# K transposed on VectorE and q in a block-diagonal stationary tile, in a decode step of attention and MLP

## The chip, the cores and the metric

One core of a Trainium2 chip runs the whole program. The time is in device microseconds, from one execution; lower is better. Weights and cache start in HBM, and each is read once.

## The reference

One token per sequence for two sequences (B = 2, D = 576). The normed token feeds two branches that are added to it: attention over the last W = 2048 keys of a cache (32 query heads, 16 key heads, head size 128), and an MLP with squared relu (F = 4608). All inputs are bf16.

```python
xn = _layernorm(x)
q = (xn @ wq) as [B, 32, 1, 128]
k, v = k_cache[:, :, Sk - W:, :], v_cache[:, :, Sk - W:, :]   # W = 2048, each key head serves 2 query heads
p = softmax(q k^T * 128 ** -0.5);  o = p v
A = o.reshape(B, 1, 4096) @ wo
h = relu(xn @ w1 + b1) ** 2;  Bout = h @ w2 + b2
return x + A + Bout
```

## The kernel before

The attention is cut into eight units `u`: four key heads of one sequence each (`NU = 8`). A unit has 2 MB of K and 2 MB of V. Both are loaded by one DMA each into a tile of 128 partitions by 8192 bf16: a partition holds 64 consecutive keys of one head (4 heads by 32 partitions). Six such tiles (`kvpool`) rotate over all K and V loads and one piece of w2; a load whose tile is still in use waits on SP's queue, with all that stands behind it. The order of loads is k0, wq, k1, v0, k2, v1, k3, v2, k4, v3, k5, v4, k6, v5, w1, k7, v6, v7, wo, then w2 in pieces (w2a, w2b, three of w2c). wq, w1 and wo share one buffer (`wbig`), so w1 waits for q and wo waits for the MLP's first product.

For each unit, `transposes(u, g)` turns K: g goes over eight groups of 1024 columns, each transposed by TensorE as f32 pairs into PSUM (`kT_ps`, three buffers, L97) and copied out in turn by ScalarE (L270) and VectorE (L272) into `kT`, half a unit (`t` = 0, 1) to a tile, with two buffers. `scores(u, t)` then takes eight matmuls for a half: a stationary tile of 32 columns cut from `qz` (q of the eight query heads with zeros around it), 512 moving columns, on four column groups of TensorE at once (`tile_position`), all summed in `sc_ps`, whose first matmul writes a mask. `softmax(u)` takes the row maximum (L291), picks own heads (L293), takes the maximum over partitions on GpSimd (L295), makes the bias (L298), the exponential on ScalarE (L302) and the transposed probabilities `pT` on VectorE (L305).

`pv(w)` multiplies by V two units later (w = u - 2), 16 matmuls on four column groups; `pv_end(w)` adds four parts of `o_ps` on VectorE (L333, L335), and its `fin` sums over partitions on TensorE (`op_ps`) and finishes in three VectorE instructions (L344, L347, L351) into `ws`. `step(u)` mixes the eight groups of unit u with `pv` of unit u - 2. TensorE's order is the program's order (L94 and L97 are the helpers that record every matmul and transpose, so go by tile names); the other engines are ordered by the scheduler. Step 1 to step 6 follow each other; then `mlp_h` with w1, step 7, `pv_all(6)` and `pv_all(7)`. The closing block sums into `out_ps`: 128 matmuls with wo, 72 with w2a, 36 with w2b and 36 with w2c.

Of the kernel before, what the change touches and what calls it, by code (L numbers as in the profile page):

```python
# [16 lines left out]
def kernel(  # L17
# [14 lines left out]
    nc = tc.nc  # L32
# [17 lines left out]
    JG = 8  # L50
    NG = NJ // JG
# [5 lines left out]
    TG = NG // NT  # L57
    QZ = 2 * NC
    assert SR == 32 and NG % NT == 0
# [35 lines left out]

    def transpose(*a, **k):
        tc.keep_in_program_order(nc.tensor.transpose(*a, **k))  # L97
# [18 lines left out]
    def issue_flat(w, name):  # L116
        n = w.shape[0] * w.shape[1] // P
        tl = wbig.tile([P, NH * L1], BF16, tag="wbig", name=name)
        nc.sync.dma_start(out=tl[:, 0:n], in_=w.rearrange("r n -> (r n)").rearrange("(p l) -> p l", p=P))
        return tl  # L120

    const.tile([P, 144], F32, name="pad_0")
# [15 lines left out]
    tmp_f = work.tile([P, 2, Dh], F32, tag="tmp", name="tmp_f")  # L138
# [50 lines left out]
    nc.vector.tensor_scalar(out=off[:], in0=own[:], scalar1=BIG, scalar2=-BIG, op0=ALU.mult, op1=ALU.add)  # L189
    of_h = const.tile([P, NC * WC], F32, name="of_h")  # L190
# [30 lines left out]
    qz = const.tile([P, NQ, B, 2, 3 * QZ], BF16, name="qz")  # L221
    nc.gpsimd.memset(qz[:], 0.0)
# [3 lines left out]
    def q_block():  # L226
        for t in range(NH):
            for g in range(NG4):
                o = t * LQ + g * QW
                matmul(q_ps[32 * g:32 * g + 2 * B, :], lhsT=xnT[:, t].rearrange("p x b -> p (x b)"),  # L230
                       rhs=wq_sb[:, o:o + QW], start=(t == 0), stop=(t == NH - 1), skip_group_check=True,
                       tile_position=(0, 32 * g))
        row_t = const.tile([RB, 4 * HW], BF16, tag="row", name="qrow")
        qrow = row_t[:, 0:2 * QW]
        nh = QH // 2
        for k in range(2):
            cp = nc.scalar.copy if k else nc.vector.tensor_copy
            cp(out=qrow[:, k * QW:(k + 1) * QW].rearrange("p (i a d) -> p i a d", a=2, d=Dh),  # L238
               in_=q_ps[0:RB, k * QW // 2:(k + 1) * QW // 2].rearrange("p (i d) -> p i d", d=Dh).unsqueeze(2)
               .to_broadcast([RB, nh, 2, Dh]))  # L240
        qrow_f = qrow.bitcast(F32)
        qT_ps = psum.tile([P, QH * P], F32, tag="sc", bufs=2, name="qT_ps")
        for i in range(QH):
            transpose(out=qT_ps[:, i * P:i * P + RB], in_=qrow_f[:, i * Dh:(i + 1) * Dh],
                      identity=ident_f[0:RB, 0:RB])
        qT_v = qT_ps[:].bitcast(BF16).rearrange("p (i g e x b c) -> p b x g c e i", g=NG4 // 2, e=2, x=32 // B, b=B, c=2)
        hd = Dh // 2
        for j2 in range(2):
            cp = nc.scalar.copy if j2 else nc.vector.tensor_copy
            pp = slice(hd * j2, hd * (j2 + 1))  # L250
            o = QZ + NC * j2
            for b in range(B):
                for half in range(2):
                    cp(out=qz[pp, half * NQ // 2:(half + 1) * NQ // 2, b, :, o:o + NC].rearrange(  # L254
                        "p g c (e i) -> p g c e i", e=2), in_=qT_v[pp, b, half])

    kT_tiles, sc_tiles, pT_tiles, o1_tiles, o_tiles = {}, {}, {}, {}, {}
    def transposes(u, g):
        k_f = k_tiles[u][:].bitcast(F32)
        kT_ps = psum.tile([P, JG * P], BF16, tag="kT", bufs=3, name=f"kT_ps_{u}_{g}")  # L260
        kT_f = kT_ps[:].bitcast(F32)
        for i in range(JG // 2):
            j = g * JG // 2 + i
            transpose(out=kT_f[:, i * P:(i + 1) * P], in_=k_f[:, j * P:(j + 1) * P], identity=ident_f[:])
        t, o = divmod(g, TG)
        if o == 0:
            kT_tiles[(u, t)] = ktpool.tile([P, TG * JG * P], BF16, tag="kT_sb", name=f"kT_{u}_{t}")
        kT = kT_tiles[(u, t)][:, o * JG * P:(o + 1) * JG * P]
        if g % 2 == 0:
            nc.scalar.copy(out=kT, in_=kT_ps[:])  # L270
        else:
            nc.vector.tensor_copy(out=kT, in_=kT_ps[:])  # L272

    def scores(u, t):
        tq, b = divmod(u, B)
        if t == 0:
            sc_tiles[u] = psum.tile([P, NJJ * 32], F32, tag="sc", bufs=2, name=f"sc_ps_{u}")
            matmul(sc_tiles[u][:], lhsT=far_h[:], rhs=is_h, start=True, stop=False, skip_group_check=True)
        sc_ps = sc_tiles[u]
        kT = kT_tiles.pop((u, t))[:].rearrange("p (j k c) -> p j k c", k=P, c=2)  # L280
        z = QZ * (1 - t)
        for c in range(2):
            for g in range(4):
                matmul(sc_ps[32 * g:32 * (g + 1), :], lhsT=qz[:, tq, b, c, z:z + SR],
                       rhs=kT[:, :, 32 * g:32 * (g + 1), c], start=False, stop=(t == NT - 1 and c == 1),
                       skip_group_check=True, tile_position=(0, 32 * g))

    def softmax(u):
        sc_ps = sc_tiles.pop(u)
        m1 = work.tile([P, 1], F32, tag="m1", name=f"m1_{u}")  # L290
        nc.vector.tensor_reduce(out=m1[:], in_=sc_ps[:], axis=AX.X, op=ALU.max)  # L291
        m2 = work.tile([P, NC], F32, tag="m2", name=f"m2_{u}")
        nc.vector.tensor_scalar(out=m2[:], in0=off[:], scalar1=m1[:, 0:1], scalar2=None, op0=ALU.add)  # L293
        gmax = work.tile([P, NC], F32, tag="gmax", name=f"gmax_{u}")
        nc.gpsimd.partition_all_reduce(gmax[:], m2[:], channels=P, reduce_op=ReduceOp.max)  # L295
        gown = work.tile([P, NC], F32, tag="gown", name=f"gown_{u}")
        bias = work.tile([P, 1], F32, tag="bias", name=f"bias_{u}")
        nc.vector.scalar_tensor_tensor(out=gown[:], in0=gmax[:], scalar=-scale, in1=own[:], op0=ALU.mult,  # L298
                                       op1=ALU.mult, accum_out=bias[:])
        p_sb = work.tile([P, NJJ * 32], BF16, tag="p_sb", bufs=1, name=f"p_{u}")  # L300
        o1 = keep.tile([P, Dh + 1], F32, tag="o1", name=f"o1_{u}")
        nc.scalar.activation(out=p_sb[:], in_=sc_ps[:], func=ACT.Exp, bias=bias[:, 0:1], scale=scale,  # L302
                             accum_out=o1[:, Dh:Dh + 1])
        pT = keep.tile([P, NJJ, SR], BF16, tag="pT", name=f"pT_{u}")
        nc.vector.transpose(out=pT[:].rearrange("p j r -> p (j r)"), in_=p_sb[:])  # L305
        pT_tiles[u] = pT
        o1_tiles[u] = o1
# [6 lines left out]
    def pv(u, part, parts):  # L314
        n = NJJ // parts
        if part == 0:
            o_tiles[u] = psum.tile([P, NS * Dh], F32, tag="o", name=f"o_ps_{u}")
        v = v_tiles[u][:].rearrange("p (t j s d) -> p j t s d", t=NT, s=2, d=Dh)
        for j in range(part * n, (part + 1) * n):
# [3 lines left out]
        if part == parts - 1:  # L323
            pT_tiles.pop(u)

    def pv_end(u):
# [3 lines left out]
        for k in range(NS):  # L330
            kw = dict(out=o1[:, 0:Dh], in0=o_ps[:, k * Dh:(k + 1) * Dh])
            if k == 0:
                nc.vector.tensor_scalar(scalar1=in_s[:, 0:1], scalar2=None, op0=ALU.mult, **kw)  # L333
            else:
                nc.vector.scalar_tensor_tensor(scalar=in_s[:, k:k + 1], in1=o1[:, 0:Dh], op0=ALU.mult, op1=ALU.add,  # L335
                                               **kw)

        def fin():
# [5 lines left out]
            nc.vector.reciprocal(out=linv[pp, :], in_=op[pp, Dh:Dh + 1])  # L344
            om_t = work.tile([P, Dh], F32, tag="om", name=f"om_{u}")
            om = om_t[pp, :].rearrange("p (q r) -> p q r", r=WR)
            nc.vector.scalar_tensor_tensor(out=om, in0=op[pp, 0:Dh].rearrange("p (q r) -> p q r", r=WR),  # L347
                                           scalar=linv[pp, 0:1], op0=ALU.mult, op1=ALU.mult,
                                           in1=own_c[pp, :].unsqueeze(2).to_broadcast([32, WC, WR]))
            with nc.allow_low_precision(reason="sums of one term and zeros"):  # L350
                nc.vector.tensor_reduce(out=ws[pp, :, BS * b], in_=om.rearrange("p q r -> p r q"), axis=AX.X,  # L351
                                        op=ALU.add)
# [3 lines left out]
    def mlp_h(w1_sb):  # L356
        h_ps = [psum.tile([P, HB], F32, tag="kT", bufs=3, name=f"h_ps_{k}") for k in range(2)]
# [29 lines left out]
    def step(u):  # L387
        fin = None
        w = u - 2
        with_pv = w >= 0  # L390
        for g in range(NG):
            transposes(u, g)
            if with_pv and g == 1:
                pv(w, 0, 2)
            if with_pv and g == 2:
                pv(w, 1, 2)
                fin = pv_end(w)
            if g == TG + 1:
                scores(u, 0)
            if g == TG + 2 and fin:  # L400
                fin()
        scores(u, 1)
        softmax(u)

    def pv_all(u):
        pv(u, 0, 1)
        pv_end(u)()

    for g in range(NG):
        transposes(0, g)  # L410
    q_block()
    for t in range(NT):
        scores(0, t)
    softmax(0)
    load_v(2)
    b1_rows = B_b1.rearrange("(x n) -> x n", n=HW)
# [4 lines left out]
    load_k(4)  # L421
# [16 lines left out]
    nc.sync.dma_start(out=w2a_sb[:], in_=w2_rows[0])  # L438
# [3 lines left out]
    step(NU - 1)  # L442
# [45 lines left out]
```

## Time and profile before

| what | value |
|---|---|
| median of 4 runs | 134.1 us (134.02 to 134.65) |
| the profiled execution | 134.12 us, span 132.2 us |
| mean granted TensorE clock | 0.827 |
| read from HBM | 53.62 MB, 406 GB/s over the span |
| busy, share of the span | TensorE 64%, its weight loads 39%, VectorE 48%, ScalarE 35%, GpSimd 4% |
| K transposes on TensorE (f32, 256) | 39.9 us |
| copies of them | ScalarE 31.9 us, VectorE 21.8 us |
| chain that ended last, by engine | DMA 77%, TensorE 17% |

A group's line reads: line of the code, engine, operation, out<-in, shapes and count; then busy us and mean ns of one; then idle us of the engine just before, with what ended most of it. A timeline line reads: start us, length us, engine, line, operation, tiles, count, and in brackets the idle time before it. The chain's lines have start, length and what. `PEld` is TensorE's weight load, `SPq` the issuing of DMAs.

### The profile page before, as it was taken

To read this page: it belongs to the slowest core of one execution; us is meant where nothing else is said; L and a number is where in the kernel's file an instruction comes from. 1 tells how busy PE (TensorE), PEld (TensorE's weight loads), DVE (VectorE), ACT (ScalarE), POOL (GpSimd) and SP (SyncE) were. 2 spreads that over 40 slices of the span, in tenths; PEclk is the share of its full clock that TensorE was granted. 3 is DMA by queue.
4 is the path that set the end of the run, shared out by engine and by line. 5 is a ranking of instruction groups with operands and counts; after the bars stand their busy time and mean duration, and the time that the engine had idled before them with its cause. 6 is when DMAs were issued, how large, how long until landed. Compare 5 with 4: busy or idle time off the path is not lost.

```text
span 132.2 us, 2285 instructions
## 1 busy us (share of the span) xinstructions
PE 84.0 (64%) x949; PEld 51.4 (39%) x949; DVE 63.0 (48%) x176; ACT 46.7 (35%) x67; POOL 4.9 (4%) x15
## 2 busy tenths in 40 slices
PE   0079219699698779687696597003919974619651
PEld 0068102258345435353353353002418631209550
DVE  7764300325549657677496576400074477560000
ACT  5717300318846366085283563200015452000000
POOL 5000000010010010100100100100000001000000
PEclk9999975556999999999999999955555899755775
DMA  4999989999999999999999999999999999899960
GB/s 159 387 447 469 424 383 431 426 441 426 421 444 411 441 426 426 431 426 446 421 444 411 426 493 401 457 411 394 441 426 436 473 429 457 382 427 401 417 246 1
DMA packets 3511, 53.76 MB, mean 407 GB/s; under 512 B 419, under 2 KB 558, under 8 KB 814
## 3 DMA queue, kind: packets, MB, share of 16 engines
q1 hardware_dynamic: 3456, 53.61, 95.1%
q8 instruction: 7, 0.11, 0.3%
q10 hardware_dynamic: 46, 0.02, 0.0%
q14 instruction: 2, 0.02, 0.0%
HBM read 53.62 MB, written 0.00 MB: 406 GB/s over the span
## 4 chain that ended last, share of the span: by engine, by line
DMA 77%; PE 17%; SPq 2%; DVE 1%; issue 1%; ACT 0%; ACTq 0%; DVEq 0%
DMA w<-in_B_w_dram 25%; DMA w2c<-in_B_w_dram 23%; DMA k<-in_A_k_cache_dram 15%; DMA wq<-in_A_wq_dram 14%; PE kT_ps L97 5%; PE h_ps L94 3%; PE q_ps L94 3%; PE sc_ps L94 2%; PE out_ps L94 1%; PE qT_ps L97 1%; SPq L106 1%; PE o_ps L94 1%; DVE qrow L238 1%; DVE qz L254 0%; SPq L438 0%
## 5 line engine op out<-in xcount | busy, mean ns | idle before, releaser
L97 PE MATMUL kT_ps<-ident_f,k 128*128 128x128 f32 x256 | 39.9, 304 | 6.1 <-DMA k<-in_A_k_cache_dram 4.0
L97 PEld LDWEIGHTS kT_ps<-ident_f,k 128*128 128x128 f32 x256 | 31.5, 156 | 19.4 <-issue 10.7
L270 ACT COPY kT<-kT_ps 128x1024 bf16<-128x1024 bf16 x32 | 31.9, 1013 | 17.3 <-PE kT_ps L97 17.2
L272 DVE COPY kT<-kT_ps 128x1024 bf16<-128x1024 bf16 x32 | 21.8, 681 | 5.7 <-PE kT_ps L97 5.5
L94 PE MATMUL sc_ps<-kT,qz 128*32 128x512 bf16 x128 | 10.5, 414 | 6.4 <-DVE kT L272 4.7
L302 ACT ACTIVATE p<-sc_ps,bias 128x512 bf16<-128x512 f32 x8 | 5.5, 687 | 21.4 <-DVE gown L298 21.3
L94 PE MATMUL o_ps<-v,pT 128*32 128x512 bf16 x128 | 10.9, 423 | 0.0
L94 PEld LDWEIGHTS <-xnT 128*4 128x4 bf16 x108 | 3.5, 121 | 18.0 <-issue 16.4
L94 PE MATMUL h_ps<-w,xnT 128*4 128x288 bf16 x72 | 4.5, 443 | 8.7 <-DMA w<-in_B_w_dram 8.7
L305 DVE STREAM_TRANSPOSE pT<-p 128x512 bf16<-128x512 bf16 x8 | 5.7, 710 | 6.1 <-ACT p L302 6.1
L335 DVE SCALAR_TENSOR_TENSOR o<-o_ps,in_s,o 128x128 f32<-128x128 f32 x24 | 8.3, 346 | 0.4
L291 DVE TENSOR_REDUCE m<-sc_ps 128x1 f32<-128x512 f32 x8 | 5.5, 692 | 5.5 <-PE sc_ps L94 5.5
L375 DVE TENSOR_TENSOR hrow<-t 100x1152 bf16<-100x1152 f32 x2 | 2.6, 1354 | 10.4 <-ACT t L373 10.4
L94 PE MATMUL q_ps<-wq,xnT 128*4 128x512 bf16 x36 | 4.0, 627 | 5.3 <-DMA wq<-in_A_wq_dram 5.3
L295 POOL PARTITION_ALL_REDUCE gmax<-m x8 | 2.9, 367 | 105.8 <-DVE m L293 105.8
L94 PE MATMUL op_ps<-o,of_h 128*32 128x129 f32 x16 | 3.4, 299 | 4.6 <-DVE o L335 4.6
L94 PEld LDWEIGHTS <-qz 128*32 128x32 bf16 x128 | 2.2, 98 | 10.6 <-DVE kT L272 7.2
L456 ACT CAST fin_sb<-out_ps 113x144 bf16<-113x144 f32 x1 | 0.3, 280 | 17.1 <-PE out_ps L94 17.1
L97 PE MATMUL pro_ps<-ident,xn_sb 2*128 2x2 bf16 x5 | 0.9, 181 | 6.8 <-DVE xn_sb L171 6.5
L238 DVE CAST qrow<-q_ps 100x512 bf16<-100x512 f32 x1 | 0.7, 693 | 8.7 <-PE q_ps L94 8.7
L94 PE MATMUL out_ps<-wo,ws 128*17 128x144 bf16 x128 | 4.0, 325 | 1.2 <-DVE ws L351 1.2
L94 PEld LDWEIGHTS <-hT_sb 128*17 128x17 bf16 x144 | 3.4, 109 | 3.2 <-issue 3.1
(71 smaller groups left out, 58.1 us busy)
## 6 DMA issues: line engine op xcount, KB each, us to landing
k<-in_A_k_cache_dram SPq DMA_DIRECT2D x8, 2048.0 KB, 20.9
v<-in_A_v_cache_dram SPq DMA_DIRECT2D x8, 2048.0 KB, 21.0
w<-in_B_w_dram SPq DMA_DIRECT2D x1, 5184.0 KB
wq<-in_A_wq_dram SPq DMA_DIRECT2D x1, 4608.0 KB, 17.9
wo<-in_A_wo_dram SPq DMA_DIRECT2D x1, 4608.0 KB
w2a<-in_B_w_dram SPq DMA_DIRECT2D x1, 2592.0 KB, 26.6
w2b<-in_B_w_dram SPq DMA_DIRECT2D x1, 1296.0 KB
w2c<-in_B_w_dram SPq DMA_DIRECT2D x1, 864.0 KB
```

Of the source, the lines that this page charges most:

```text
L94: tc.keep_in_program_order(nc.tensor.matmul(*a, **k))
L97: tc.keep_in_program_order(nc.tensor.transpose(*a, **k))
L106: nc.sync.dma_start(out=tl[:], in_=cache[b, tq * TH:(tq + 1) * TH, S0:Sk, :].rearrange("h (c j) d -> c h (j d)", c=CP))
L238: cp(out=qrow[:, k * QW:(k + 1) * QW].rearrange("p (i a d) -> p i a d", a=2, d=Dh), in_=q_ps[0:RB, k * QW // 2:(k + 1) * QW // 2].rearrang ...
L270: nc.scalar.copy(out=kT, in_=kT_ps[:])
L272: nc.vector.tensor_copy(out=kT, in_=kT_ps[:])
L291: nc.vector.tensor_reduce(out=m1[:], in_=sc_ps[:], axis=AX.X, op=ALU.max)
L295: nc.gpsimd.partition_all_reduce(gmax[:], m2[:], channels=P, reduce_op=ReduceOp.max)
L302: nc.scalar.activation(out=p_sb[:], in_=sc_ps[:], func=ACT.Exp, bias=bias[:, 0:1], scale=scale, accum_out=o1[:, Dh:Dh + 1])
L305: nc.vector.transpose(out=pT[:].rearrange("p j r -> p (j r)"), in_=p_sb[:])
L335: nc.vector.scalar_tensor_tensor(scalar=in_s[:, k:k + 1], in1=o1[:, 0:Dh], op0=ALU.mult, op1=ALU.add, **kw)
L375: nc.vector.tensor_tensor(out=h4[:, :, k * HB:(k + 1) * HB], in0=t4, in1=t4, op=ALU.mult)
```

## The change

K is no longer transposed by TensorE. `transposes(u, t)` is one VectorE instruction for half a unit: a transpose in blocks of 32 by 32 of the same f32 pairs, from the K tile straight into `kT`, with no PSUM and no copy. What comes out keeps four blocks of partitions (the four heads) apart, so the stationary tile changes: `qc` holds q laid out for four quarters of the head dimension, and once per unit `q_place(u)` multiplies it by a mask on VectorE into `qz[u % 2]`, a tile with one block per head on its diagonal. `scores` then takes eight matmuls for a half with 128 stationary columns (no `tile_position`), shifted by 8 columns for each quarter of a partition's keys. V is cut to match.

The order changes too. Nearly all of VectorE's instructions are now kept in program order (`dve`). In `step(u)` the next unit's q and its first half are transposed before unit u's maximum, and its second half between the exponential and `pT` (so unit u's own halves were done in step u - 1). Unit 7 is not prepared ahead: its step starts with q and both halves. `pv` is no longer split. Unit 0 goes through `step(0)`; k4 is written ahead of step 1 in the code, and the order of loads on SP's queue is as before. The MLP's `h_ps` has its own two PSUM buffers.

```diff
-    def transposes(u, g):
-        k_f = k_tiles[u][:].bitcast(F32)
-        kT_ps = psum.tile([P, JG * P], BF16, tag="kT", bufs=3, name=f"kT_ps_{u}_{g}")
-        kT_f = kT_ps[:].bitcast(F32)
-        for i in range(JG // 2):
-            j = g * JG // 2 + i
-            transpose(out=kT_f[:, i * P:(i + 1) * P], in_=k_f[:, j * P:(j + 1) * P], identity=ident_f[:])
...
-        if g % 2 == 0:
-            nc.scalar.copy(out=kT, in_=kT_ps[:])
-        else:
-            nc.vector.tensor_copy(out=kT, in_=kT_ps[:])
+    def transposes(u, t):
+        kT = ktpool.tile([P, UE // NT], BF16, tag="kT_sb", name=f"kT_{u}_{t}")
+        n = UE // NT // 2
+        tc.keep_in_program_order(nc.vector.transpose(out=kT[:].bitcast(F32),
+                                                     in_=k_tiles[u][:].bitcast(F32)[:, t * n:(t + 1) * n]))
+        kT_tiles[(u, t)] = kT
...
+    def q_place(u):
+        tq, b = divmod(u, B)
+        sh = [P, NA, NP4, NC]
+        dve(nc.vector.tensor_tensor(out=qz[u % 2][:, :, QO:].rearrange("p a (q c) -> p a q c", c=32)[:, :, :, 0:NC],
+                                    in0=qc[:, tq, b].unsqueeze(2).to_broadcast(sh),
+                                    in1=own_p[:].unsqueeze(1).unsqueeze(3).to_broadcast(sh), op=ALU.mult))
...
-        for c in range(2):
-            for g in range(4):
-                matmul(sc_ps[32 * g:32 * (g + 1), :], lhsT=qz[:, tq, b, c, z:z + SR],
-                       rhs=kT[:, :, 32 * g:32 * (g + 1), c], start=False, stop=(t == NT - 1 and c == 1),
-                       skip_group_check=True, tile_position=(0, 32 * g))
+        for i in range(NS // NT):
+            z = QO - NC * (t * NS // NT + i)
+            for h in range(2):
+                for e in range(2):
+                    matmul(sc_ps[:], lhsT=qz[u % 2][:, 2 * h + e, z:z + P], rhs=kT[:, i, :, h, :, e], start=False,
+                           stop=(t == NT - 1 and i == NS // NT - 1 and h == 1 and e == 1), skip_group_check=True)
...
-    def step(u):
-        fin = None
+    def step(u, ahead=True):
         w = u - 2
-        with_pv = w >= 0
-        for g in range(NG):
-            transposes(u, g)
-            if with_pv and g == 1:
-                pv(w, 0, 2)
-            if with_pv and g == 2:
-                pv(w, 1, 2)
-                fin = pv_end(w)
-            if g == TG + 1:
-                scores(u, 0)
-            if g == TG + 2 and fin:
-                fin()
-        scores(u, 1)
-        softmax(u)
+        if not ahead:
+            q_place(u)
+            for t in range(NT):
+                transposes(u, t)
+        if w >= 0:
+            pv(w)
+        for t in range(NT):
+            scores(u, t)
+        fin = pv_end(w) if w >= 0 else None
+        nxt = u + 1 < NU - 1
+        if nxt:
+            q_place(u + 1)
+            transposes(u + 1, 0)
+        rest = softmax(u)
+        if fin:
+            fin()
+        rest(transposes if nxt else None, u + 1)
```

`softmax(u)` now stops after the maximum over partitions, and `rest` does the bias, the exponential, the next unit's second half (`between`) and `pT`.

## The prediction

> **What bounds the kernel now.** I read the queue table and the rates first, because a kernel that moves 53.6 MB in 132 us may have little else to win.
>
> ```profile
> DMA  4999989999999999999999999999999999899960
> ...
> q1 hardware_dynamic: 3456, 53.61, 95.1%
> q8 instruction: 7, 0.11, 0.3%
> ```
>
> The load queue keeps 16 engines 95.1% busy from the second slice to the last but one. Windows of 2 us show 389 to 459 GB/s from 30 to 74 us, with TensorE at work, and a mean of 412 from 84 to 90, where it sits still: no engine's work lowers the rate. Next the chain that ended last, in order of time:
>
> ```profile
> 58.12 33.14 DMA w<-in_B_w_dram
> 91.26 0.04 issue
> 91.30 4.52 PE h_ps L94 x72
> ...
> 97.16 30.80 DMA w2c<-in_B_w_dram
> 127.97 0.04 issue
> 128.01 1.45 PE out_ps L94 x36
> ```
>
> From 58 us on it is two loads and what waits for them. The attention units run beside it. Their margin stands in the issues: k takes a median of 20.9 us from issue to landing, of which one load's own share is about 4.9 us (k lands at 54.61, 64.4 and 74.3: two loads in 9.9). Some 16 us of other loads lie ahead of each new one, so an issue may come that much later before an engine runs dry. The end has far less margin, and there I read the timeline of TensorE:
>
> ```profile
> 119.04 4.02 PE L94 MATMUL out_ps<-wo,ws 128*17 128x144 bf16 x128 [1.16 <-DVE ws L351]
> 122.88 1.57 PE L94 MATMUL out_ps<-w2a,hT_sb 128*17 128x144 bf16 x54
> 125.96 0.48 PE L94 MATMUL out_ps<-w2a,hT_sb 128*17 128x144 bf16 x18 [1.52 <-issue]
> 126.22 0.78 PE L94 MATMUL out_ps<-w2b,hT_sb 128*17 128x144 bf16 x36
> 128.01 1.42 PE L94 MATMUL out_ps<-w2c,hT_sb 128*17 128x144 bf16 x36 [1.00 <-DMA w2c<-in_B_w_dram]
> ```
>
> The closing 272 matmuls start when VectorE has finished the last unit (L351), and reach the last load with only 1.52 + 1.00 us of waiting in them. That is all the cover the last unit has.
>
> **Removed, added, moved: units 0 to 6.** These rows price them:
>
> ```profile
> L97 PE MATMUL kT_ps<-ident_f,k 128*128 128x128 f32 x256 | 39.9, 304 | 6.1 <-DMA k<-in_A_k_cache_dram 4.0
> ...
> L270 ACT COPY kT<-kT_ps 128x1024 bf16<-128x1024 bf16 x32 | 31.9, 1013 | 17.3 <-PE kT_ps L97 17.2
> L272 DVE COPY kT<-kT_ps 128x1024 bf16<-128x1024 bf16 x32 | 21.8, 681 | 5.7 <-PE kT_ps L97 5.5
> ...
> L305 DVE STREAM_TRANSPOSE pT<-p 128x512 bf16<-128x512 bf16 x8 | 5.7, 710 | 6.1 <-ACT p L302 6.1
> ```
>
> TensorE loses 39.9 us of transposes, ScalarE 31.9 us of copies and VectorE 21.8 us. All of it lay beside the loads, so it is worth nothing by itself. VectorE gains two transposes of 128x2048 f32 per unit, of which no row exists. Rows near it: 128x32 f32 in 0.16 us and 128x512 bf16 in 0.71. The line through both gives 2.46 us; if a four-byte column costs twice a two-byte one, 2 x 4 x 0.71 = 5.7 us. The f32 row lies below the bf16 line rather than above it, so I take 2.46 and keep 5.7 as a rival. VectorE per unit then: 4.9 for K, 0.71 pT, 0.69 maximum, 0.23, 0.25 bias, 4 x 0.35 for o, 0.9 for the three of `fin`, 0.35 for q (as L347, also two inputs and 128 columns): 9.4 us against 9.9 us of loads.
>
> Scores keep 16 matmuls of 512 columns per unit, but with 128 stationary columns instead of 32 they no longer run four at a time. From o_ps at full clock, 16 packed in 1.03 us and 8 in 0.62: one pass is 0.41 / 2 = 0.205 us; at half clock (16 scores in 1.90, 8 of o_ps in 1.04) it is 0.43. So 3.3 or 6.9 us per unit; with o_ps, op_ps and the mask 5.1 or 9.8, again within 9.9 and off VectorE's path, since VectorE transposes the next half meanwhile. The Trainium skill, "TensorEngine Tiling (Array Packing)", Performance Considerations, speaks against the change here: a stationary of 32 columns should be packed, for up to four times. The 0.62 us for eight agrees with it, and the change gives that up; on a TensorE that drops 39.9 us the page's factor costs nothing in units 0 to 6, and the sum would stay.
>
> q costs more once: two casts of 1024 columns for 512 (0.7 and 0.6 us more), four more transposes (0.3 each) and unit 0's 16 passes at half clock (6.9 for 1.9). k1 becomes free at about 39 us, not 34.65. k4 keeps its place on SP's queue. It and each later issue (v3 to w1 and what stands behind them) move by 2 to 5 us against 16 us of cover: nothing; without that cover it would be those 2 to 5 us. The new waits of VectorE (kT's two buffers until the scores have read them, q's tile until the unit before last) fall behind passes that end earlier. Behind the transpose that waits for a K load stands the unit's maximum; K is there by 5 us or more. After unit 6, w1 at 91.26 still gates `mlp_h`, and wo is issued at 95.8 with 10 us of k7, v6 and v7 still queued.
>
> **The last unit is where it shows.** VectorE's last hT copy ends at 101.83. Then come q (0.3) and both transposes of unit 7: kT is complete at 104.6 and 107.05, where TensorE used to do this interleaved. The scores' first 8 passes run to about 108, the second 8 to 109.9 (full clock) or 111.6 (half). The clock came back at 103.5 in the rows of before; with a gap ahead of 104.6 I take it in between: the maximum at 110.5 instead of 109.76, 0.7 late.
>
> From there the order is fixed by hand, and this is how it went before:
>
> ```profile
> 109.76 0.69 DVE L291 TENSOR_REDUCE m<-sc_ps 128x1 f32<-128x512 f32 x1 [0.27 <-PE sc_ps L94]
> ...
> 111.38 0.35 DVE L333 TENSOR_SCALAR o<-o_ps,in_s 128x128 f32<-128x128 f32 x1
> 111.76 0.74 DVE L335 SCALAR_TENSOR_TENSOR o<-o_ps,in_s,o 128x128 f32<-128x128 f32 x2
> 112.42 0.70 DVE L305 STREAM_TRANSPOSE pT<-p 128x512 bf16<-128x512 bf16 x1
> ```
>
> Unit 6's o (L333, L335) ran while ScalarE did the exponential. Now it stands behind pT, and the three of unit 5's `fin` stand ahead of the bias. New chain: 0.69 + 0.23 + 0.9 + 0.1 of gaps to the bias; 1.13 to pT (111.29 to 112.42); 0.74; o of unit 6 1.5; 0.15; op and o_ps of unit 7 2.1 (113.50 to 115.58), for TensorE is in order; then 3.42 as before (115.62 to 119.04). That is 11.0 us against 9.28. The closing block starts at 110.5 + 11.0 = 121.5, 2.5 us late.
>
> Against 2.5 us of waits this gives nothing if both waits give way, and 1.5 us if the 1.52 us stays. That wait is "issue": it falls after 54 of the 72 matmuls of w2a, not at a change of tile, and the trace has an instruction packet of 16 KB from 123.49 to 124.45. The other reading is w2b's landing at 125.9. The Trainium skill, "Runtime: NRT & Kernel Launch", Instruction fetch mechanics, says that instructions come in blocks of 16 KiB fetched ahead and that crossing one is mostly hidden. By the page the stall is none, and the sum would be 134.1; the row of 1.52 us speaks for one that is not hidden where small matmuls follow fast. I give the stall two thirds: +1.0 us. The profiled execution took 134.12 for a span of 132.2, as good as the median of 134.1, so 135.1.
>
> **Rivals.** *Cover holds:* the last load still ends the kernel, 134.1. For it: 2.5 late against 2.5 of waits. Against: nothing is left over.
>
> *Faster:* instruction packets share the 16 engines, and seven of them can leave some engines behind. From 126.5 us on the half-microsecond windows show 348, 261, 171, 118 and 18 GB/s; the 0.46 MB in them would take 1.1 us at 420 and takes 2.5. The new kernel issues fewer TensorE instructions (256 transposes and their weights gone), perhaps five packets. Between 2/7 of 1.4 = 0.4 us and all of it: 132.7 to 133.7, say 133.4. It decides only if the closing block starts before about 120.3.
>
> *Transposes at 5.7 us:* VectorE then needs 9.4 + 2 x 3.24 = 15.9 us per unit against 9.9; seven units lose 42 us, less 16 of cover: 26 us, 160. At 4 us each (12.5 per unit) it is 18 - 16 = 2 us. It decides from about 3.8 us per transpose.
>
> **How the numbers follow.** 0.5% is 0.67 us, about what a measurement of this kernel can tell. Forecast 64%, from 134.1 to 136.0: 48 above 134.8, 16 within. Cover holds 12%, within. Faster 14%: 10 beyond, 4 within. Slow transposes 10%, slower. So slower 0.58, same 0.32, faster 0.10. The range 133.4 to 137.0 leaves out half of the faster case and most of the slow transposes.
>
> **What would show it.** Right: the 128x2048 transposes near 2.4 us; no wait for a K load behind which the load queue runs dry; w1's landing still near 91.3; the maximum of unit 7 near 110.5, the first wo matmul near 121.5, and no wait for w2c before the last 36. Wrong: a wait of 1 us for w2c as now (cover held), a last landing well before 128 (faster), or w1 landing after 95 (the queue ran dry).

## The result, and the profile after

The changed kernel takes 134.31 us (median, 134.05 to 135.24), the kernel before 134.04 (133.85 to 134.8): a ratio of 1.0019, 95% interval 1.0013 to 1.0024. It is slower, by 0.25 us. The forecast had the direction, though by luck, as the section on the prediction shows, and 135.1 us was 0.8 too much: it had put +1.0 us on a change that costs a quarter of that. The profiled execution took 134.32 us for a span (from the first recorded instruction to the last) of 132.2, the same span as before.

On the page of after, VectorE has gone from 63.0 to 80.7 us, TensorE from 84.0 to 73.1, ScalarE from 46.7 to 15.8, and the loads keep their share:

```profile
PE 73.1 (55%) x697; PEld 32.6 (25%) x697; DVE 80.7 (61%) x169; ACT 15.8 (12%) x35; POOL 5.3 (4%) x16
...
q1 hardware_dynamic: 3456, 53.61, 95.1%
q8 instruction: 5, 0.08, 0.2%
...
L94 PE MATMUL sc_ps<-kT,qz 128*128 128x512 bf16 x128 | 36.0, 432 | 17.2 <-DVE kT L271 17.0
L271 DVE STREAM_TRANSPOSE kT<-k 128x2048 f32<-128x2048 f32 x16 | 36.6, 2299 | 5.9 <-PE sc_ps L94 3.5
```

The new transpose takes 2.30 us, and TensorE's scores wait for it 17.0 us in all; nothing hurries them there except in unit 7, where 1.67 us of it fall. The load queue is as full as it was.

The chain that ended last (start, length, what) shows both ends of the story. The load of w1 is still in it and lands at the same time as before; behind w1 it is now compute to the end, with no load in it:

```profile
56.14 35.10 DMA w<-in_B_w_dram
91.28 4.27 PE h_ps L94 x68
...
101.92 2.23 DVE kT L271
104.20 6.39 PE sc_ps L94 x16
110.61 0.70 DVE m L291
...
121.34 5.58 PE out_ps L94 x178
126.91 0.80 issue
127.71 1.69 PE out_ps L94 x94
```

The hand-written order in unit 7 stands on VectorE's timeline as the prediction read it: `fin` of unit 5 ahead of the bias (L300), unit 6's o behind pT (L309).

```profile
110.61 0.69 DVE L291 TENSOR_REDUCE m<-sc_ps 128x1 f32<-128x512 f32 x1 [2.74 <-PE sc_ps L94]
...
112.19 0.37 DVE L354 TENSOR_REDUCE ws<-om 32x32 bf16<-32x128 f32 x1
112.59 0.17 DVE L300 SCALAR_TENSOR_TENSOR gown<-gmax,own 128x8 f32<-128x8 f32 x1
...
113.69 0.71 DVE L309 STREAM_TRANSPOSE pT<-p 128x512 bf16<-128x512 bf16 x1 [0.93 <-ACT p L304]
114.43 0.35 DVE L336 TENSOR_SCALAR o<-o_ps,in_s 128x128 f32<-128x128 f32 x1
```

The closing block on TensorE's and ScalarE's timeline of after:

```profile
121.34 4.02 PE L94 MATMUL out_ps<-wo,ws 128*17 128x144 bf16 x128 [1.16 <-DVE ws L354]
125.13 1.78 PE L94 MATMUL out_ps<-w2a,hT_sb 128*17 128x144 bf16 x50
127.71 0.55 PE L94 MATMUL out_ps<-w2a,hT_sb 128*17 128x144 bf16 x22 [0.80 <-issue]
128.04 0.79 PE L94 MATMUL out_ps<-w2b,hT_sb 128*17 128x144 bf16 x36
128.60 0.79 PE L94 MATMUL out_ps<-w2c,hT_sb 128*17 128x144 bf16 x36
129.43 0.28 ACT L460 CAST fin_sb<-out_ps 113x144 bf16<-113x144 f32 x1 [15.77 <-PE out_ps L94]
```

It starts 2.30 us later than before, its stall is 0.80 us instead of 1.52, the wait of 1.00 us for w2c is gone, and the result is copied out at 129.43. In before that row reads

```profile
129.48 0.28 ACT L456 CAST fin_sb<-out_ps 113x144 bf16<-113x144 f32 x1 [17.12 <-PE out_ps L94]
```

So inside the span of the profiled execution nothing was lost. The last load landed at 129.05 (before 129.09). Over all runs the same holds in the main: the median span is 132.1 us for both kernels, but 6 of 52 runs of after have a span of 132.4 to 133.0, where none of 104 of before goes over 132.3.

### The profile page after: what moved, and what is told of

The parts are those of the page before. It is cut to its first block, busy times and chain, and to the rows that moved or that the text cites. A ratio compares the mean times of both kernels' runs of the same rounds, so it can differ in the third digit from the quotient of the medians.

```text
span 132.2 us, 1735 instructions
## 1 busy us (share of the span) xinstructions
PE 73.1 (55%) x697; PEld 32.6 (25%) x697; DVE 80.7 (61%) x169; ACT 15.8 (12%) x35; POOL 5.3 (4%) x16
## 4 chain that ended last, share of the span: by engine, by line
DMA 40%; DVE 26%; PE 23%; issue 5%; ACT 2%; SPq 1%; POOL 1%; ACTq 0%
DMA w<-in_B_w_dram 27%; DMA wq<-in_A_wq_dram 13%; DVE kT L271 11%; PE sc_ps L94 8%; PE out_ps L94 5%; PE h_ps L94 3%; PE q_ps L94 3%; DVE o L338 3%; DVE hrow L378 2%; DVE pT L309 2%; PE o_ps L94 2%; DVE m L291 2%; DVE qrow L245 1%; DVE o L336 1%; PE op_ps L94 1%
## 5 line engine op out<-in xcount | busy, mean ns | idle before, releaser
L94 PE MATMUL sc_ps<-kT,qz 128*128 128x512 bf16 x128 | 36.0, 432 | 17.2 <-DVE kT L271 17.0
L271 DVE STREAM_TRANSPOSE kT<-k 128x2048 f32<-128x2048 f32 x16 | 36.6, 2299 | 5.9 <-PE sc_ps L94 3.5
L94 PEld LDWEIGHTS <-qz 128*128 128x128 bf16 x128 | 13.3, 105 | 37.9 <-issue 27.2
L94 PE MATMUL o_ps<-v,pT 128*32 128x512 bf16 x128 | 13.0, 486 | 0.0
L245 DVE CAST qrow<-q_ps 100x1024 bf16<-100x1024 f32 x1 | 1.2, 1226 | 10.0 <-PE q_ps L94 10.0
L309 DVE STREAM_TRANSPOSE pT<-p 128x512 bf16<-128x512 bf16 x8 | 5.4, 676 | 1.9 <-ACT p L304 1.9
L94 PEld LDWEIGHTS <-pT 128*32 128x32 bf16 x128 | 4.5, 110 | 3.1 <-issue 1.8
L94 PEld LDWEIGHTS <-ws 128*17 128x17 bf16 x128 | 3.7, 135 | 1.6 <-issue 1.6
L94 PEld LDWEIGHTS op_ps<-o,of_h 128*32 128x32 f32 x16 | 1.2, 119 | 11.5 <-issue 9.4
L94 PE MATMUL sc_ps<-ident,far_h 4*128 4x512 bf16 x8 | 3.6, 445 | 0.0
```

Of the source, the lines that this page charges most:

```text
L94: tc.keep_in_program_order(nc.tensor.matmul(*a, **k))
L245: cp(out=qrow[:, h * 2 * QW:(h + 1) * 2 * QW].rearrange("p (i a d) -> p i a d", a=NP4, d=HD), in_=q_v[:, h].unsqueeze(2).to_broadcast([RB, ...
L271: tc.keep_in_program_order(nc.vector.transpose(out=kT[:].bitcast(F32), in_=k_tiles[u][:].bitcast(F32)[:, t * n:(t + 1) * n]))
L309: dve(nc.vector.transpose(out=pT[:].rearrange("p j r -> p (j r)"), in_=p_sb[:]))
```

## Experiments

All ratios are to the kernel before, run beside each on the same chip (its median there 134.03 to 134.07).

**e1_after_tail and e2_before_late: is it the late block?** e1 gives after the last unit's order of before; e2 gives before the late block of after.

```diff
 e1, in step(u) of after, for unit 7:
+        if not ahead:
+            pv(u - 1)
+            fins = [fin]
+            rest(lambda v, t: fins.append(pv_end(v)), u - 1)
+            for f in fins:
+                f()
+            return
...
-    pv_all(NU - 2)
 e2, in pv_end(u) of before, six more instructions of 0.35 us:
-        for k in range(NS):
+        for k in ((0, 1) * 3 if u == NU - 1 else ()) + tuple(range(NS)):
```

> Unit 7's softmax puts o of unit 6 between the exponential and pT, and unit 5's three last instructions behind pT, near the order of before; nothing else differs from the changed kernel. Theory (late closing block): wo's first matmul moves from 121.3 to about 120.2, the wait for w2c comes back, and the time falls by 0.1 to 0.3 us to that of before (134.0 to 134.2; ratio 1.000 to 1.001). Rival (the extra 0.25 us comes from the units before, or from the loads): the block starts 1 us earlier and the time stays at 134.3, ratio 1.002. Prediction on record (the stall stays 1.5 us): falls by a full 1.1 us or to the last load.

> The kernel before with six more VectorE additions of 0.37 us in unit 7's o, so that the closing block starts 2.25 us later (121.3); K stays on TensorE. Theory: the same 0.2 to 0.3 us as the whole change, ratio 1.0015 to 1.0025. Rival (the closing block has cover left, the 0.25 us is from elsewhere): ratio 1.000. Prediction on record (2.5 us of waits of which 1.5 stay): 1.0 us or more, ratio over 1.007.

e1 took 134.24 us, 1.0012 (1.0002 to 1.0022); e2 133.96, 0.9993 (0.9984 to 1.0001). TensorE's timeline, first e1, then e2:

```profile
118.87 3.82 PE L94 MATMUL out_ps<-wo,ws 128*17 128x144 bf16 x128 [1.16 <-DVE ws L354]
...
125.19 0.55 PE L94 MATMUL out_ps<-w2a,hT_sb 128*17 128x144 bf16 x23 [1.41 <-issue]
...
127.96 0.55 PE L94 MATMUL out_ps<-w2c,hT_sb 128*17 128x144 bf16 x24 [1.33 <-DMA w2c<-in_B_w_dram]
```

```profile
120.76 4.02 PE L94 MATMUL out_ps<-wo,ws 128*17 128x144 bf16 x128 [1.16 <-DVE ws L351]
...
127.44 0.48 PE L94 MATMUL out_ps<-w2a,hT_sb 128*17 128x144 bf16 x18 [1.22 <-issue]
...
128.26 1.00 PE L94 MATMUL out_ps<-w2c,hT_sb 128*17 128x144 bf16 x36
```

e1 starts its block 2.5 us earlier than after and gives it back in waits, most of it for w2c; e2 starts 1.7 us later than before and loses nothing. My theory after the result, that the late block costs the 0.25 us, falls.

**e3_after_late: how much later may it start?** After with e2's six instructions in its own `pv_end`.

> The changed kernel with the same six additions: the closing block starts at 123.6. Theory (the change has used up all cover): the time rises by 2.0 to 2.3 us, to 136.3 to 136.6. Rival (some cover is left, for the stall shrinks when data and instructions are there): by 0.5 to 1.5 us.

135.58 us, 1.0115 (1.0094 to 1.0136). The block starts at 122.66 and the copy-out at 130.80:

```profile
122.66 3.38 PE L94 MATMUL out_ps<-wo,ws 128*17 128x144 bf16 x128 [1.16 <-DVE ws L354]
125.87 0.99 PE L94 MATMUL out_ps<-w2a,hT_sb 128*17 128x144 bf16 x50
129.08 0.55 PE L94 MATMUL out_ps<-w2a,hT_sb 128*17 128x144 bf16 x22 [2.23 <-issue]
```

The block starts 1.32 us later than in after, and the end comes 1.37 later. From here each us counts in full: after's profiled execution sits on the edge of its cover. The start was expected at 123.6; the scores of unit 7 took 5.32 us in this execution and 6.38 in after's, so it came earlier, and the rise of 1.27 us in the time lies in the rival's range. The first 178 matmuls ran faster here (3.38 and 0.99 for 4.02 and 1.78), and the stall grew by as much.

**e4_after_shift: is the stall instruction fetch, or w2b?** After with 24 small matmuls in TensorE's wait for wq, so that every later instruction stands 48 places further on.

```diff
+    dum = psum.tile([P, Dh + 1], F32, tag="op", name="dum")
+    for _ in range(24):
+        matmul(dum[0:MB, 0:Dh], lhsT=ident[:, 0:MB], rhs=ident[:], start=True, stop=True, skip_group_check=True)
```

> The changed kernel with 24 small extra matmuls (128x17 by 128 columns, result unused) while TensorE waits for wq at 8 to 19 us. Theory (the stall of 0.80 us in the closing block is the fetch of the next block of instructions): it moves with the count of instructions, from after 178 matmuls of the block to after about 154, whatever tile they read. Rival (it waits for the landing of w2b): it stays at the same place, after 178. Time: unchanged within 0.2 us in both.

134.24 us, 1.0017 (0.9999 to 1.0035). The stall comes 24 matmuls earlier, after 26 of w2a and not 50; w2b's tile is not in play there:

```profile
124.01 0.61 PE L94 MATMUL out_ps<-w2a,hT_sb 128*17 128x144 bf16 x26
126.31 0.92 PE L94 MATMUL out_ps<-w2a,hT_sb 128*17 128x144 bf16 x46 [1.69 <-issue]
```

It is tied to the place in the stream: instruction fetch. e13, further down, moves it the other way: its 504 rows more are two blocks of 256 less 8, and the stall comes 4 matmuls later than in after, as its expectation says:

```profile
124.37 1.24 PE L94 MATMUL out_ps<-w2a,hT_sb 128*17 128x144 bf16 x54
127.43 0.48 PE L94 MATMUL out_ps<-w2a,hT_sb 128*17 128x144 bf16 x18 [1.82 <-issue]
```

In e4, before, after and e1 to e3 a packet of 16 KB on the instruction queue starts 2.27 to 2.49 us before TensorE goes on. The stall reads as what is left of that time when the instructions already there are used up.

**e5_after_act15, e6_before_act85, e7_tail_act15: the part outside the span.** With equal spans, the 0.25 us must lie around them. Time less span, median over the runs, is 2.16 us for after and 1.90 for before. Past the span's end after has an instruction packet of 8 KB, before has none; I took it for ScalarE's closing code. The edit is small copies that feed nothing and run on ScalarE before q comes:

```diff
+        for k in range(3):      # 17 in e6; for u = 2 to 6
+            nc.scalar.copy(out=pad_t[0:2, 3 * u + k:3 * u + k + 1], in_=eps_t[0:2, 0:1])
```

> After, with 15 copies of one element by two partitions added on ScalarE in its wait for q (they feed nothing). In the profiles the time is 2.16 us above the span for after and 1.91 for before, at equal spans, and queue 14 moves an 8 KB packet 1.8 us past the end of after's span, where before has one at 69.14 us, when ScalarE had 67 rows recorded; after's ScalarE has 59 rows in all. Theory 'late fetch': the last packet is ScalarE's next block of instructions, needed by its closing code, and costs about 0.25 us outside the span. With 74 rows it comes in mid-kernel: the packet at 133.9 us is gone, time less span falls to 1.9 us, and the time is 134.0 to 134.1 us (ratio 0.999 to 1.0005). Rival 'not ScalarE' or 'packet costs nothing': time less span stays 2.1 to 2.2 and the time 134.25 to 134.35 (1.002).

> Before, with 85 such copies on ScalarE in its wait for q, which bring its recorded rows from 105 to 190. If a block is 128 rows and the first ends at row 67, the next ends at row 195, inside the closing code. Theory 'late fetch': an 8 KB packet of queue 14 appears some 1.8 us after the span's end, time less span rises from 1.9 to 2.15 us, and the time is 134.25 to 134.35 us (ratio 1.001 to 1.0025). Rival: ratio 1.000, time less span 1.9. If the copies delay q by some us, the units have some 16 us of cover for that and the end does not move.

> The kernel of e1_after_tail (last unit in before's order) with the 15 copies of e5_after_act15. If the two effects are separate and add, e1's 134.24 loses the same 0.25 us: 134.0 us, ratio 0.9985 to 1.000. If e1 had already taken the part that e5 takes, e7 equals e1, 1.001. If the copies do nothing, also 1.001.

The packet went where the theory said: in e5 from 133.97 to 116.29 us, in e6 a new one at 133.11, a us behind the end. The time did not follow: time less span 2.17 in e5, 1.87 in e6, 2.16 in e7 (134.28 us, 1.0015, 1.0005 to 1.0025). The theory falls; that packet costs nothing. e5's 134.67 us (1.0039, 1.0020 to 1.0059) and its span are another matter: its profile has the block start at 121.86 and the copy-out at 129.90, over the edge that e3 showed by 0.5 us, and 5 of its 8 runs have a span of 132.4 or more. Why it starts late so often, no run shows.

**e8_after_dup1 and e15_after_dup2: the cover of units 0 to 6.** The transposes of units 1 to 6 done twice, first halves only in e8, both in e15.

```diff
-        tc.keep_in_program_order(nc.vector.transpose(...))
+        for _ in range(2 if 0 < u < NU - 1 and t == 0 else 1):      # e15: without t == 0
+            tc.keep_in_program_order(nc.vector.transpose(...))
```

> After, with the first-half transpose of units 1 to 6 done twice (the second writes the same values): 2.3 us more on VectorE per unit, 13.8 us in all. Theory 'loads bound the units': VectorE's step grows from about 8.7 to 11.0 us against 9.9 us of loads for a unit, the debt over six units is some 7 us and the cover 16, so the time stays at 134.2 to 134.5 (1.001 to 1.003), with w1's first matmul still set by its landing. Rival 'VectorE is the bound in the units': each unit costs 2.3 us more, 13.8 in all, 148 us (1.10).

> After, with both halves' transposes of units 1 to 6 done twice: 4.6 us more on VectorE per unit, 27.6 us in all. e8_after_dup1 added 13.8 us and moved the end of unit 6 by 9.5 and the closing block by 0.8. Theory 'VectorE is the bound once the 7.7 us of wait for w1 is used up': the further 13.8 us come through whole, closing block some 14 us later than e8's, time 148 to 150 us. Rival 'the loads still absorb part of it': 140 to 146.

e8 took 135.41 us, 1.0121 (1.0090 to 1.0151), which was not expected; e15 149.75, 1.1167 (1.1085 to 1.1249), as expected. The first `mlp_h` matmul, the bias's, comes at 83.21 us in after, 93.73 in e8 and 109.06 in e15; after waits 7.67 us for w1 behind it, e8 no more. The closing blocks start at 122.16 and 136.94. e8 and e15, their rows of w1:

```profile
93.73 0.41 PE L94 MATMUL h_ps<-b_sb,sel_h 8*128 8x288 bf16 x2
94.07 2.38 PE L94 MATMUL h_ps<-w,xnT 128*4 128x288 bf16 x72
```

```profile
109.06 0.41 PE L94 MATMUL h_ps<-b_sb,sel_h 8*128 8x288 bf16 x2
109.41 2.38 PE L94 MATMUL h_ps<-w,xnT 128*4 128x288 bf16 x72
```

Of 13.8 us added, 2.8 reach w1's matmul (94.07 against 91.28); of 27.6, 18.1 do. The cover is 9.5 to 11 us, not 16, and behind it VectorE is the bound: the second 13.8 us move w1's matmul by 15.3. In e8 the closing block is only 0.8 us late, for w1's 72 matmuls take 2.38 us there, at a granted clock of 1.00, and 4.49 in after, at 0.50. The cover is mostly the wait for w1. Ahead of it VectorE has little to spare: from 31 to 83.2 us it is busy for 47.6 of 52.2 us in after, and its two longest waits for another engine or a load from unit 0's scores on are these (engine, line, what it waited for: us, times, longest):

```profile
DVE kT L271 <- PE sc_ps L94: 3.5, 1, 3.5
DVE kT L271 <- DMA k<-in_A_k_cache_dram: 2.0, 2, 1.2
```

The first of them is over at 30.98 us, which leaves 2.0 us for K in the units. So what is added to VectorE comes out at the end of unit 6 nearly whole, 10.5 of 13.8 us, whatever is queued on SP. (In the expectation of e15 the 9.5 for unit 6 should be 10.5, by the row of the bias.)

**e9 to e12: whose stream sets the part outside?** Runs with more VectorE rows had shown less time outside the span. The edits are memsets that feed nothing, two or four on VectorE (e9, e12, e10), one on GpSimd (e11).

```diff
+    for k in range(2):      # 4 in e10_before_dve4
+        nc.vector.memset(pad_t[0:2, k:k + 1], 0.0)
 e11:
+    nc.gpsimd.memset(pad_t[0:2, 0:1], 0.0)
```

> After, with two memsets of 2x1 added on VectorE early in the kernel (they feed nothing): 186 rows recorded on it instead of 184. The four kernels with 184 show 2.12 to 2.17 us of time above the span, before with 186 shows 1.90, two with 190 show 2.02, one with 192 shows 1.75. Theory 'length of VectorE's stream': what lies outside the span goes by where VectorE's stream ends, whatever the other engines run; with 186 it is 1.90 us and the time 134.0 to 134.1. Rival 'another engine' (GpSimd has one row more in after, TensorE 503 fewer): 2.1 to 2.2 us as in after, 134.3.

> Before, with four memsets of 2x1 on VectorE: 190 rows instead of 186. Theory 'length of VectorE's stream': time above the span 2.02 us as in the two kernels with 190 rows, 134.15 to 134.25. Rival 'another engine': 1.90, 134.05; rival 'six more rows take 0.15 us off any kernel': about 1.80.

> Before, with one memset of 2x1 on GpSimd: 36 rows on it as in after. Theory 'length of VectorE's stream': unchanged, 1.90 us above the span, 134.05. Rival 'GpSimd's row': 2.15 us, 134.3.

> The kernel of e1_after_tail with the two memsets of e9_after_dve2 (186 rows on VectorE). Theory 'length of VectorE's stream': 1.90 us above the span at a span of 132.1, 134.0 us, ratio 0.999 to 1.000: all that separated e1 from before is gone. Rival: 134.24 as e1, 1.0012.

**e13_after_pe252 and e14_tail_both** add 252 matmuls of 16 columns in the wait for wq, as in e4, so that TensorE's stream is as long as in before. In the table below, rows are all that the trace records of an engine; a matmul and its weight load are one each.

> After, with 252 matmuls of 16 columns on TensorE in the wait for wq (they feed nothing): about 1913 rows recorded on TensorE, as in before (1912), instead of 1409. Theory 'length of TensorE's stream': the part of the 0.25 us outside the span that VectorE's rows do not explain follows TensorE's; time above the span falls from 2.16 to 1.9 or 2.0 us, the time to 134.05 to 134.15. Rival 'neither': 2.16, 134.3. The 504 rows are 8 short of two blocks of 256, so the stall in the closing block moves by 4 matmuls at most; a start later than 121.3 adds what it is late.

> The kernel of e1_after_tail with the 252 matmuls of e13_after_pe252 and the two memsets of e9_after_dve2. Theory 'streams': both parts go, 1.85 to 1.95 us above the span, 134.0 us (ratio 0.999 to 1.0005). Rival: only VectorE's part goes, 2.05 us as e12_tail_dve2, 134.15.

| kernel | rows of VectorE, TensorE | us (ratio, interval) | time less span |
|---|---|---|---|
| before | 186, 1912 | 134.03 to 134.07 | 1.90 |
| e10: before, 4 on VectorE | 190, 1912 | 133.99 (0.9988, 0.9974 to 1.0003) | 1.83 |
| e2: before, 6 on VectorE | 192, 1912 | 133.96 (0.9993, 0.9984 to 1.0001) | 1.75 |
| e11: before, 1 on GpSimd | 186, 1912 | 134.03 (1.0005, 0.9989 to 1.0020) | 1.92 |
| e6: before, 85 on ScalarE | 186, 1912 | 134.07 (1.0002, 0.9993 to 1.0012) | 1.87 |
| after | 184, 1409 | 134.31 (1.0019, 1.0013 to 1.0024) | 2.16 |
| e1: after, before's order in unit 7 | 184, 1410 | 134.24 (1.0012, 1.0002 to 1.0022) | 2.16 |
| e9: after, 2 on VectorE | 186, 1409 | 134.15 (1.0003, 0.9991 to 1.0016) | 2.02 |
| e13: after, 252 on TensorE | 184, 1913 | 134.28 (1.0013, 1.0000 to 1.0026) | 2.14 |
| e12: e1, 2 on VectorE | 186, 1410 | 134.15 (1.0012, 1.0003 to 1.0022) | 2.05 |
| e14: e1, 252 and 2 | 186, 1914 | 134.06 (0.9996, 0.9982 to 1.0010) | 1.98 |

More rows on VectorE take 0.07 to 0.15 us off in either kernel (e9, e10, e2, e12). The theory as stated falls all the same: it said 1.90 for e9, 2.02 for e10, 1.90 for e12 and up to 1.95 for e14, and they came at 2.02, 1.83, 2.05 and 1.98. At the same 186 rows after keeps 0.12 us more than before, so VectorE's rows account for half of the difference. Six rows (e3, e8: 2.03 and 2.01 us, 190 rows) do no more in after than two. Rows on ScalarE and GpSimd change nothing beyond 0.03 us, and TensorE's 504 nothing by themselves (e13). Where the other half of the 0.25 us sits stays open, as does why VectorE's rows matter: the first rows of both traces agree to 0.01 us, and from the copy-out to the span's end both take 2.76 us. The medians also hide a spread: in 16 of 104 runs of before the time less span is 2.27 to 2.58 us, in none of after over 2.26, so by the mean the difference is 0.19 us and not 0.26. Of the variants of after, e14 equals before; none is shown to beat it.

## Why the prediction was right or wrong

*Units 0 to 6 cost nothing: right, by a thinner cover than stated.* w1 landed at 91.24 us (91.26 before), the transpose took 2.30 us for 2.46, and the rivals with 5.7 us or a dry queue are out. TensorE's scores, no longer four at a time, took 36.0 us for 10.5 and cost nothing there, as said. By the two f32 rows, 32 columns in 0.16 us and 2048 in 2.30, a column costs 1.06 ns over a fixed 0.13 us; the bf16 row, 512 columns in 0.71 us, gives 1.13 ns over the same fixed part. So f32 pays no second pass, and the doubling in my 5.7 us does not come about. The Trainium skill, "Vector Engine (DVE) Microarchitecture Reference", The reshape front-end and per-opcode configuration, states for the transpose mode that it sustains one element per cycle per lane, and names no type there. These rows agree in that both types cost the same per element; how long a cycle is, no run here shows. My reason for 2.46 was not sound, though: one bf16 row makes no line for the f32 row to lie below, so that the smaller figure came true is in part luck. The issues on SP did not move by 2 to 5 us either: k4's came at 37.05 us for 34.65, and from k5 on they were earlier, w1's at 56.14 for 58.12. The 16 us of cover were read from the loads' queueing; e8 and e15 put it at 9.5 to 11 us. What was overlooked is that VectorE has hardly a gap in the units, so that an excess of its own is not absorbed by the queue but only by the 7.67 us that TensorE waits for w1 and by VectorE's few waits.

*The last unit: right.* Maximum at 110.61 (said: 110.5), chain to the first wo matmul 10.7 us (said: 11.0), block at 121.34 (said: 121.5), and w2c no longer waited for. That it fits to 0.2 us is in part luck: in the profiles of e4, e9, e13 and e5, whose unit 7 is the same code, the block starts at 120.31, 120.43, 120.58 and 121.86 us, and the scores of unit 7 take 4.98 to 6.41 us. The granted clock came back at different times: in after it is 0.50 from 104 to 108 us and 1.00 from 110, in e13 1.00 from 108.

*The closing block: the step that failed.* The prediction let 7.9 us of work stand (10.44 us from 119.04 to 129.48, less 2.52 of waits) and kept two thirds of 1.52 us as stall, so that a block from 121.5 us would end 1.0 us late, at 130.4. Measured, it ended at 129.43. Of the difference of 1.0 us the start gave 0.16, the stall 0.21 (0.80 instead of 1.01), and the work 0.63 (7.92 said; 8.09 less 0.80, 7.29 measured). The work shrank in its last 36 matmuls, 0.79 us for 1.42, and the windows of before and of after from 128.0 to 129.5 us (us, TensorE busy, granted clock, DMA share, GB/s) show why:

```profile
128.00:129.50 1.50, 1.42 (x36) 0.50 0.13 45
```

```profile
128.00:129.50 1.50, 1.39 (x90) 1.00 0.12 39
```

In before the clock had fallen to half by then, in after it stood at full. I had carried the 1.42 us over as if a matmul's price were fixed, though the prediction prices the scores at two clocks elsewhere. In before the half clock cost next to nothing, since the last landing held the end: the copy-out came 0.39 us behind it, and 0.33 in e1 and e2. Put together, most runs read simply: where the block starts after 121.3 us, the copy-out follows 8.0 to 8.1 us later (after, e3, e5, e8); where it starts earlier, 0.3 to 0.4 us behind the last landing. The exception is e15, whose block has no stall and takes 7.1 us to the copy-out at 144.08:

```profile
136.94 4.02 PE L94 MATMUL out_ps<-wo,ws 128*17 128x144 bf16 x128 [1.16 <-DVE ws L355]
140.73 2.17 PE L94 MATMUL out_ps<-w2a,hT_sb 128*17 128x144 bf16 x72
```

In the two profiled executions the cover is about 2.3 us, and the change used 2.30; where unit 7 came earlier, as in e4, e9 and e13, 0.7 to 1.0 us were left.

*The stall as fetch: right* (e4, e13). The Trainium skill, "Runtime: NRT & Kernel Launch", Instruction fetch mechanics, calls the crossing of a 16 KiB block mostly hidden. In the closing block it is not, with 0.80 us in after and 2.23 in e3. That it "stays" was right in kind; its length was taken as fixed and is not: the block's own pace decides it, and when the packet starts.

*Cover holds* (134.1) was the nearest rival: inside the span it is what happened. *Faster* failed although the instruction packets fell from seven to five as said: the last landing moved by 0.04 us. Neither they nor the forecast named the 0.25 us outside the span, which are nearly the whole of the measured difference: the prediction took the time outside the span over from before as a fixed amount, and it is 0.26 us more by the median. So the block, for which the forecast said slower, gave nothing, and the direction was had by luck. Of what makes the difference, e9 and e12 show 0.11 to 0.14 us to go with VectorE's rows; the rest stays open.

## What to carry to other kernels

Price a tail by two dates, not by its waits: when the last load lands, and when its first instruction starts plus what the block takes at the clock it will have; the later one ends the kernel, and a delay is free exactly up to where they meet. When the span does not change and the time does, compare time less span over many runs before looking for a cause inside the trace. For cover ahead of an engine, add work to that engine and see when it comes out, rather than reading the age of the queue.

## What was not expected of the hardware

A fetch of 16 KB of instructions takes TensorE about 2.4 us from the start of the packet to the next matmul in the closing block, so a burst of small matmuls stalled the longer the faster it ran up to the place: 2.23 us in e3, 0.80 in after. When the packet starts is not fixed: 3.9 us into the block in after, 1.5 in e15, which shows no stall. Why, no run here tells. An 8 KB block for ScalarE a us or two past the span costs nothing (e5, e6). Two memsets of 2x1 on VectorE took 0.14 us off the time outside the span (e9; 0.11 in e12).
